# State-by-weight products two quarters at a time beside the scores, and the first batch's first product in plain fp32

## The chip, the cores and the metric

The kernel runs on one core of one Trainium2 chip. The metric is device time in microseconds (us) of one execution; a kernel's time is the median of its runs. Before the change three runs gave 1366.35, 1363.53 and 1366.42 us, a median of 1366.35. The profile shown here is of one more execution, which took 1365.6 us and has a span of 1363.8 us.

## The reference

Two attentions read from each other, and their outputs pass through two gated feed-forward blocks. The weights arrive as 64-bit floats, so the kernel converts them itself.

```python
# x: 8 batches, 8 heads, 512 rows, 64 wide; state: the same with 32 rows
scores = x @ state.T / 8;   a  = softmax(scores);   xread = a @ state
scores2 = state @ x.T / 8;  a2 = softmax(scores2);  sread = a2 @ x
t = concat(xread, sread)                 # per batch 544 rows of 512
h = ((t @ w1) * (t @ w2)) @ w3           # w1, w2: 512 x 1024; w3: 1024 x 1024
y = h @ w_out                            # w_out: 1024 x 512
out = (sigmoid(y @ w_gate) * (y @ w_val)) @ w_out2   # 1536 wide inside
```

## The kernel before

**Split products.** Most products run in the format fp32r, one pass over the moving operand. To keep fp32 accuracy each operand is split into a high part (ACT copies it into an fp32r tile) and a low part (DVE subtracts the high part from the original); `split` (line 65) does both. A product is then three matmuls: high by high, high by low, low by high (`products`, line 114).

**First feed-forward block.** It never forms `xread` for the 512 rows. With `aT` the softmax over the states, transposed, `xread @ w1` is `aT.T` times (state times w1). So for each batch `StateWeights.make(q)` (line 370) multiplies the state by one quarter `q` of w1 and w2: 16 small matmuls of 64 rows by 32 columns that lie side by side in the array (tile `psw`), followed by a split into the tiles `sw`. Two consecutive blocks `j` of `ffn1` (line 444) use one quarter. For each of 8 blocks `j`, `ffn1` forms the two products `pab` (128x512, from `aT` and `sw`), multiplies them (line 470) and splits the result into `u`. Then four products `py` (d = 0 to 3) multiply all `u` by `wp`, which is w3 times w_out, formed once in the first batch (`wp_step`, line 425, tile `pwp`, with transposes of w3 in `pw`).

**The front.** In the first batch everything waits for weights: `convert` (line 332) and `cvt` (line 71) load 64-bit tiles into three buffers `raw`, and ACT and DVE turn each into 32-bit numbers. w1 and w2 take 16 such tiles, w_out 8, w3 16. The converted quarters of w1 and w2 are also written to memory and fetched again for each later batch (`fetch`, tile `wq`, 1 MB each, two buffers).

**What sets the order.** The order on PE is the order in which the program is written (line 160). `ffn1` has slots, 0 to 7 ahead of the blocks `j` and 8 to 11 ahead of `d`, and lines 622 to 673 hang work into them: the next batch's transposes of x (`pxt`), scores (`psc`, `scores`, line 190), softmax (`soft1` to `soft3`, which end in the split of `aT`), the quarters 0 and 1 of the next batch (slots 9 and 10; in the first batch 8 and 11), its quarters 2 and 3 (slots 0 and 3 of the next batch). In the first batch `wp_step(0)` stands in slot 7, ahead of the last block `j`, and the other seven in slot 8. The other engines are ordered by the scheduler. `psw` shares two PSUM tiles (`ps_at`) with the transposes and scores.

**The rest.** After the eighth batch the state rows follow, and then the second feed-forward block, which takes the time from about 585 us to the end.

Of the kernel before, what the change touches and what calls it, by code (L numbers as in the profile page):

```python
# [8 lines left out]
F32 = mybir.dt.float32  # L9
# [12 lines left out]
def tile_state_attention__then__gated_ffns(  # L22
# [137 lines left out]
    with tc.manual_schedule(engines={mybir.EngineType.PE}):  # L160
# [5 lines left out]
        def load_x(b, pool):  # L166
            t = pool.tile([P, G, SC, 2, D], F32, name="xn", bufs=1)
# [6 lines left out]
        def attention(b):  # L174
# [61 lines left out]
            def soft3():  # L236
# [5 lines left out]
                )  # L242
                aT[b] = [at.tile([P, 2, S], F32R, name=f"aT{i}") for i in range(2)]
# [116 lines left out]
        class StateWeights:  # L360
# [9 lines left out]
            def make(self, q):  # L370
                w = self.raw.pop(q)
                b = self.b
                pts = [ps_at.tile([P, 512], F32, tag="at", name="psw") for _ in range(2)]
                for a in range(2):
                    for g in range(G):
                        for k in range(2):
                            nc.tensor.matmul(
                                pts[k][NS * g : NS * g + NS, a * WQ : (a + 1) * WQ],
                                stT[64 * k : 64 * k + 64, g, b * NS : (b + 1) * NS],
                                w[64 * k : 64 * k + 64, a, g],  # L380
                                start=True,
                                stop=True,
                            )
                t = [pb.tile([P, 2, 2, WQ], F32R, name=f"sw{i}", bufs=3) for i in range(2)]
                for k in range(2):
                    split(*[v[:, k].rearrange("p a f -> p (a f)") for v in t], pts[k])
                self.done[q] = t

            def weights(self, j):
                t = self.done[j // 2]  # L390
                f0 = j % 2 * P
                return [[t[i][:, :, a, f0 : f0 + P] for i in range(2)] for a in range(2)]

        order = list(range(B))
        before, after = attention(order[0])
        nxt = StateWeights(order[0])
        stages = [fn for i in sorted(before) for fn in before[i]]
        nxt.raw[0] = convert(0, {1: lambda: load_x(order[0], at)})
# [3 lines left out]
        wo = [pw.tile([P, JF, DM], F32R, name=f"wo{i}", bufs=1) for i in range(2)]  # L402

        def wo_step(k):
            split(wo[0][:, k], wo[1][:, k], cvt(w_out[k * P : (k + 1) * P, :], cv))
# [19 lines left out]
        def wp_step(f):  # L425
# [3 lines left out]
            if f + 1 < JF:  # L429
# [6 lines left out]
                        ([t[:, k % 4] for t in w3t[2 * f + k // 4]], [t[:, k] for t in wo])  # L436
# [7 lines left out]
        def ffn1(c, n, kblocks, weights, xin, slots):  # L444
# [6 lines left out]
            for j in range(JF):  # L451
# [4 lines left out]
                for ab in range(2):  # L456
# [11 lines left out]
                asb = pb.tile([P, 512], F32, name="asb")  # L468
                p2["act"] = copy("act", asb[:, :n], pab[0][:, :n])
                p2["dve"] = nc.vector.tensor_tensor(  # L470
                    out=asb[:, :n], in0=asb[:, :n], in1=pab[1][:, :n], op=ALU.mult
                )
                uj = [pu.tile([P, 512], F32R, name=f"u{i}", bufs=JF) for i in range(2)]
                split(uj[0][:, :n], uj[1][:, :n], asb[:, :n])
                u.append(uj)
# [18 lines left out]
        class DirectWeights:  # L494
# [5 lines left out]
            def prep(self, j):  # L500
# [4 lines left out]
                t = [pb.tile([P, 2, KM, P], F32R, tag=f"sw{i}", name=f"dw{i}", bufs=3) for i in range(2)]  # L505
# [115 lines left out]

        for t, b in enumerate(order):
            cur = nxt
            slots = {i: [] for i in range(JF + KM)}
            if t == 0:
                for q in range(NQ):
                    slots[2 * q].append(lambda q=q, cur=cur: cur.make(q))
# [9 lines left out]
                for f in range(JF):  # L637
                    slots[min(JF, f + WS)].append(lambda f=f: wp_step(f))
# [11 lines left out]
            if t + 1 < B:  # L650
                if t == 0:
                    slots[JF].append(lambda: behind(lambda: load_x(order[1], pu)))
                else:
                    go = lambda t=t: load_x(order[t + 1], at if t % 2 else pu)
                    slots[0].insert(0, (lambda go=go: behind(go)) if t == 1 else go)
                before, after = attention(order[t + 1])
                nxt = StateWeights(order[t + 1])
                for i, fns in before.items():
                    slots[i + 2 if t == 0 else i] += fns
                for q in range(2):  # L660
                    if t == 0:
                        slots[JF].append(lambda q=q, nxt=nxt: behind(lambda: nxt.fetch(q)))
                    else:
                        slots[4].append(lambda q=q, nxt=nxt: nxt.fetch(q))
                    i = (8, 11)[q] if t == 0 else 9 + q
                    slots[i].append(lambda q=q, nxt=nxt: nxt.make(q))
                    slots[i].append(lambda q=q, nxt=nxt: nxt.fetch(q + 2))
# [5 lines left out]
            ffn1(t, S, 2, cur.weights, aT[b], slots)  # L673
# [488 lines left out]
```

## Time and profile before

| | before |
|---|---|
| median of 3 runs | 1366.35 us |
| the profiled execution, its time and its span | 1365.6 us, 1363.8 us |
| PE busy | 1311.1 us (96%) |
| DVE busy, ACT busy | 857.5 us (63%), 681.9 us (50%) |
| end of w3 times w_out, first batch | 143.6 us |
| one later batch (scores to scores) | 54.2 us |

PE is the engine that matters: from about 89 us to the end it hardly ever stands still. Ahead of that it waits for weights. The clock that the throttle granted to PE is 1.00 (the level of 2.4 GHz) in nearly every slice of the span, and lower only between 40 and 100 us.

### The profile page before, as it was taken

To read this page: it belongs to the slowest core of one execution; us is meant where nothing else is said; L and a number is where in the kernel's file an instruction comes from. 1 tells how busy PE (TensorE), PEld (TensorE's weight loads), DVE (VectorE), ACT (ScalarE), POOL (GpSimd) and SP (SyncE) were. 2 spreads that over 40 slices of the span, in tenths; PEclk is the share of its full clock that TensorE was granted. 3 is DMA by queue.
4 is the path that set the end of the run, shared out by engine and by line. 5 is a ranking of instruction groups with operands and counts; after the bars stand their busy time and mean duration, and the time that the engine had idled before them with its cause. 6 is when DMAs were issued, how large, how long until landed. Compare 5 with 4: busy or idle time off the path is not lost. (4 is left out here: it accounts for less than half of the span.)

```text
span 1363.8 us, 20423 instructions
## 1 busy us (share of the span) xinstructions
PE 1311.1 (96%) x7696; PEld 1100.9 (81%) x7696; DVE 857.5 (63%) x1528; ACT 681.9 (50%) x1344; POOL 132.4 (10%) x155
## 2 busy tenths in 40 slices
PE   3769999999999999999999999999999999999997
PEld 1558777777777777988889998888999988889996
DVE  6776354645645558348658776768777756557643
ACT  6775344454544556355646655635545533424431
POOL 0000000010110111002122211121211000000000
PEclk9879999999999999999999999999999999999999
DMA  7847433454464444454244377454465654042222
GB/s 221 296 162 219 138 106 124 125 154 178 143 213 155 155 160 181 182 219 166 101 155 150 133 262 247 184 199 156 164 213 191 237 218 156 28 159 93 82 93 70
DMA packets 125354, 224.68 MB, mean 165 GB/s; under 512 B 44104, under 2 KB 71240, under 8 KB 118600
## 3 DMA queue, kind: packets, MB, share of 16 engines
q1 hardware_dynamic: 90088, 162.95, 35.7%
q10 hardware_dynamic: 33440, 46.80, 10.2%
q0 software_dynamic: 1728, 13.63, 2.5%
q8 instruction: 60, 0.98, 0.3%
q14 instruction: 38, 0.31, 0.1%
HBM read 155.19 MB, written 68.16 MB: 164 GB/s over the span
## 5 line engine op out<-in xcount | busy, mean ns | idle before, releaser
L949 PE MATMUL psA<-y,wt 128*128 128x384 f32 (+1 forms) x1440 | 300.9, 357 | 0.6 <-ACT sg L974 0.5
L1046 PE MATMUL po<-wo,p 128*128 128x512 f32 x1224 | 281.0, 390 | 0.7 <-DVE p L602 0.7
L949 PEld LDWEIGHTS psA<-y,wt 128*128 128x128 f32 x1440 | 259.0, 188 | 24.9 <-DVE sg L985 0.9
L1046 PEld LDWEIGHTS po<-wo,p 128*128 128x128 f32 x1224 | 229.3, 188 | 49.0 <-DVE p L602 1.8
L949 PE MATMUL psB<-y,wt 128*128 128x384 f32 (+1 forms) x720 | 159.6, 356 | 0.0
L123 PE MATMUL pab<-aT,sw 128*128 128x512 f32 x512 | 149.3, 414 | 10.3 <-ACT aT L62 6.6
L62 ACT ACTIVATE u<-psA 128x384 f32<-128x384 f32 (+1 forms) x120 | 63.9, 532 | 156.1 <-PE psA L949 141.5
L949 PEld LDWEIGHTS psB<-y,wt 128*128 128x128 f32 x720 | 130.0, 188 | 11.2
L123 PE MATMUL py<-u,wp 128*128 128x512 f32 (+1 forms) x576 | 133.3, 383 | 1.1 <-DVE u L67 0.6
L123 PEld LDWEIGHTS py<-u,wp 128*128 128x128 f32 x576 | 102.4, 188 | 32.5 <-issue 9.2
L123 PEld LDWEIGHTS pab<-aT,sw 128*128 128x128 f32 x512 | 95.2, 195 | 36.9 <-ACT aT L62 7.5
L62 ACT ACTIVATE p<-sg 128x384 fp32r<-128x384 f32 (+1 forms) x120 | 68.0, 567 | 81.1 <-DVE sg L985 69.8
L67 POOL TENSOR_TENSOR o<-m,o 128x256 fp32r<-128x256 f32 x72 | 60.2, 836 | 435.1 <-ACT o L62 379.8
L470 DVE TENSOR_TENSOR asb<-asb,pab 128x512 f32<-128x512 f32 (+1 forms) x72 | 47.3, 657 | 71.5 <-PE pab L126 61.2
L1061 DVE TENSOR_TENSOR ob<-po,ob 128x512 f32<-128x512 f32 x68 | 46.7, 688 | 63.4 <-PE po L1046 60.2
L976 DVE TENSOR_TENSOR sg<-psB,u 128x384 f32<-128x384 f32 (+1 forms) x60 | 36.4, 607 | 75.1 <-ACT u L62 75.0
L126 PE MATMUL pab<-aT,sw 128*128 128x512 f32 x256 | 81.3, 399 | 0.0
L949 PE MATMUL psC<-y,wt 128*128 128x384 f32 (+1 forms) x360 | 80.2, 357 | 0.0
L67 DVE TENSOR_TENSOR sw<-psw,sw 128x512 fp32r<-128x512 f32 x64 | 41.5, 680 | 56.7 <-ACT sw L62 56.6
L602 DVE TENSOR_TENSOR p<-sg,p 128x384 fp32r<-128x384 f32 (+1 forms) x120 | 73.8, 615 | 3.9 <-ACT p L62 0.8
L602 DVE TENSOR_TENSOR y<-yf,y 128x384 fp32r<-128x384 f32 (+1 forms) x112 | 68.5, 635 | 12.0 <-ACT y L62 10.9
L67 DVE TENSOR_TENSOR u<-asb,u 128x512 fp32r<-128x512 f32 (+1 forms) x72 | 51.8, 719 | 33.5 <-ACT u L62 33.5
(114 smaller groups left out, 1783.2 us busy)
## 6 DMA issues: line engine op xcount, KB each, us to landing
wq<-w12d SPq DMA_DIRECT2D x32, 1024.0 KB, 5.0
wt<-wd SPq DMA_DIRECT2D x12, 1792.0 KB, 9.0
part<-ob SPq DMA_DIRECT2D x68, 256.0 KB, 2.6
ob<-part SPq DMA_DIRECT2D x68, 256.0 KB, 3.8
raw<-in_moe_w SPq DMA_DIRECT2D x32, 512.0 KB, 4.8
wd<-o ACTq DMA_DIRECT2D x56, 256.0 KB, 2.2
yf<-yd SPq DMA_DIRECT2D x27, 384.0 KB, 3.8
yf<-yd SPq DMA_DIRECT2D x19, 512.0 KB, 5.2
```

Of the source, the lines that this page charges most:

```text
L62: return nc.scalar.activation(out=o, in_=i, func=AF.Copy)
L67: (sub or nc.vector).tensor_tensor(out=lo, in0=src, in1=hi.bitcast(F32), op=ALU.subtract)
L123: nc.tensor.matmul(o, w[i], xx[k], start=n == 0 and i + k == 0, stop=False)
L126: nc.tensor.matmul(o, w[1 - late], xx[late], start=False, stop=n == len(pairs) - 1)
L470: p2["dve"] = nc.vector.tensor_tensor(out=asb[:, :n], in0=asb[:, :n], in1=pab[1][:, :n], op=ALU.mult)
L602: nc.vector.tensor_tensor(out=o, in0=x0, in1=x1, op=ALU.subtract)
L949: nc.tensor.matmul(o, w[:, i, kb * P : (kb + 1) * P], xx[kb][h], start=start, stop=i == 1 and kb == 1, skip_group_check=True,)
L976: nc.vector.tensor_tensor(out=t, in0=o, in1=kept[a, what], op=ALU.add)
L1046: nc.tensor.matmul(o, pt[j][i][:, s * P : (s + 1) * P], wot[j][:, h], start=j == js[0] and i + h == 0, stop=j == js[-1] and i == 1,)
L1061: nc.vector.tensor_tensor(out=ob, in0=o, in1=ob, op=ALU.add)
```

## The change

The quarters are made two at a time. In a later batch quarters 0 and 1 follow the scores in slot 8 and quarters 2 and 3 stand in slot 10; all four are ready before the next batch begins. In the first batch quarters 0 and 1 stand in slot 8 behind w3 times w_out, and quarters 2 and 3 in slot 10 behind the scores. Their PSUM tiles come from `ps_main` (four tiles), which `pab` and `pwp` use, and there are four buffers for `sw` rather than three. Fetches go in pairs as well.

For the first batch the state-by-weight tiles and `aT` are left unsplit (`plain`): each `pab` product is two plain fp32 matmuls instead of six fp32r ones, and ACT and DVE copy one `psw` tile each. The product `u` of a block stays whole in `uw`, and its split is put behind all eight `wp_step`, which now stand together in slot 8. x has two buffers in one pool, and the low parts of w_out use the buffers of `sw1`.

```diff
+        if len(groups[0][1][0][0]) == 1:
+            for o, pairs in groups:
+                for n, ((w,), (xx,)) in enumerate(pairs):
+                    nc.tensor.matmul(o, w, xx, start=n == 0, stop=n == len(pairs) - 1)
+            return
...
+                if plain:
+                    aT[b] = [tr]
+                    return
                 aT[b] = [at.tile([P, 2, S], F32R, name=f"aT{i}") for i in range(2)]
                 split(aT[b][0], aT[b][1], tr)
...
-            def make(self, q):
+            def make(self, *qs, plain=False):
...
+                    pool, tag = (ps_y, "y") if plain else (ps_main, "m")
+                    pts = [pool.tile([P, 512], F32, tag=tag, name="psw") for _ in range(2)]
...
+                    if plain:
+                        t = [pb.tile([P, 2, 2, WQ], F32, tag="sw0", name="swp", bufs=4)]
+                        for k, eng in enumerate(("act", "dve")):
+                            copy(eng, t[0][:, k].rearrange("p a f -> p (a f)"), pts[k])
...
+                keep_ = postponed is not None and j < JF - 1
+                whole = (pu.tile([P, 512], F32, tag="u", name="uw", bufs=2 * JF) if keep_ else asb)[:, :n]
...
+                if postponed is not None:
+                    postponed.append(split_u)
+                else:
+                    split_u()
...
                 for f in range(JF):
-                    slots[min(JF, f + WS)].append(lambda f=f: wp_step(f))
+                    slots[JF].append(lambda f=f: wp_step(f))
+                slots[JF].append(lambda: [fn() for fn in postponed])
...
-            if t:
-                slots[0].append(lambda cur=cur: cur.make(2))
-                slots[3].append(lambda cur=cur: cur.make(3))
...
+                    slots[JF].append(lambda nxt=nxt: nxt.make(0, 1))
+                    slots[JF].append(lambda get=get: get(2, 3))
+                    for i, fns in before.items():
+                        slots[i + 2] += fns
+                    slots[JF + 2].insert(1, lambda nxt=nxt: nxt.make(2, 3))
+                else:
+                    slots[0].append(lambda get=get: get(0, 1))
...
+                    slots[JF].insert(1, lambda nxt=nxt: nxt.make(0, 1))
+                    slots[JF].append(lambda get=get: get(2, 3))
+                    slots[JF + 2].append(lambda nxt=nxt: nxt.make(2, 3))
```

PE in the first batch, around the last block `j` (its weights are `sw_597` before, `swp` now; `pw` is a transpose of w3, `pwp` w3 times w_out). Before:

```order
L260 MATMUL psr<-xn,a2tr 32x64 x32
...
L126 MATMUL pab<-aT_223,sw_598 128x512 x2
L310 MATMUL pt<-ident,z 128x128 x4
L421 MATMUL pw_748<-ident,m 128x128 x4
L421 MATMUL pw_766<-ident,m 128x128 x4
L421 MATMUL pw_784<-ident,m 128x128 x4
...
L126 MATMUL pwp<-wo_227,w3t_772 128x512 x4
L123 MATMUL pab<-aT_223,sw_597 128x512
...
L421 MATMUL pw_850<-ident,m 128x128 x4
```

After the change (two matmuls for each `pab`):

```order
L268 MATMUL psr<-xn,a2tr 32x64 x32
L122 MATMUL pab<-a2tr,swp 128x512 x4
L318 MATMUL pt<-ident,z 128x128 x4
L438 MATMUL pw_667<-ident,m 128x128 x4
L438 MATMUL pw_685<-ident,m 128x128 x4
L438 MATMUL pw_703<-ident,m 128x128 x4
L128 MATMUL pwp<-wo_223,w3t_672 128x512
...
L131 MATMUL pwp<-wo_223,w3t_691 128x512 x4
L438 MATMUL pw_748<-ident,m 128x128 x4
```

The last block's products moved ahead of the first transposes of w3, and no `pab` stands between the sets of `pwp` any more.

PE in a later batch, from the scores on (`psc`; `py` is a product with `wp`). Before, one set of `psw` stands alone at each place:

```order
L126 MATMUL pab<-aT_1439,sw_1624 128x512 x2
L199 MATMUL psc<-xT,stT 32x512 x8
L123 MATMUL py<-u_1547,wp_82 128x512
...
L126 MATMUL py<-u_1798,wp_83 128x512
L377 MATMUL psw<-wq,stT 32x256 x16
```

After:

```order
L131 MATMUL pab<-aT_1443,sw_1398 128x512 x2
L204 MATMUL psc<-xT,stT 32x512 x8
L387 MATMUL psw<-wq,stT 32x256 x32
L128 MATMUL py<-u_1505,wp_82 128x512
...
L131 MATMUL py<-u_1728,wp_83 128x512
```

Two sets of 16 follow the scores without another product in between; the two others stand together in front of d = 2.

DVE in the first batch, from the scores of the second on (`st` and `m` belong to the softmax, `aT` ends it, `sw` is the low part of a quarter). Before:

```order
L223 TENSOR_REDUCE m_1399<-st 128x32
...
L224 TENSOR_TENSOR st<-st,m_1399 128x1024
...
L231 TENSOR_REDUCE s_1432<-st 128x32
...
L234 TENSOR_TENSOR st<-st,m_1431 128x1024
L67 TENSOR_TENSOR sw_1462<-psw,sw_1461 128x512
L240 STREAM_TRANSPOSE a2tr<-st 128x1024
...
L67 TENSOR_TENSOR aT_1440<-a2tr,aT_1439 128x1024
```

After:

```order
L67 TENSOR_TENSOR sw_1374<-psw,sw_1373 128x512
...
L228 TENSOR_REDUCE m_1403<-st 128x32
...
L67 TENSOR_TENSOR sw_1398<-psw,sw_1397 128x512 x2
L229 TENSOR_TENSOR st<-st,m_1403 128x1024
L236 TENSOR_REDUCE s_1436<-st 128x32
...
L239 TENSOR_TENSOR st<-st,m_1435 128x1024
L245 STREAM_TRANSPOSE a2tr<-st 128x1024
L67 TENSOR_TENSOR aT_1444<-a2tr,aT_1443 128x1024
```

Four subtractions of `sw` now stand ahead of the softmax's own subtraction (`st<-st,m`), where before two stood behind it.

## Rows read from the trace of the kernel before

**Rows 1.** The page, part 1: busy time of each engine, its share, instructions.
```profile
PE 1311.1 (96%) x7696; PEld 1100.9 (81%) x7696; DVE 857.5 (63%) x1528; ACT 681.9 (50%) x1344; POOL 132.4 (10%) x155
```

**Rows 2.** Busy time by stretch (count), then PE's granted clock, DMA share, GB/s.
```profile
33.00:89.00 56.00, 36.28 (x266) 26.70 (x267) 45.82 (x92) 41.20 (x73) 1.82 (x3) 0.83 0.73 249
89.00:97.00 8.00, 8.00 (x29) 6.47 (x28) 5.73 (x12) 5.57 (x9) 0.00 (x0) 0.71 0.64 221
97.00:144.00 47.00, 47.00 (x237) 39.40 (x236) 26.88 (x51) 23.48 (x41) 0.00 (x0) 1.00 0.69 203
```

**Rows 3.** Waits up to 145 us: PE's line, who ended it; total, times, longest.
```profile
PE pw L421 <- DVE m L112: 7.9, 3, 6.0
PE psr L260 <- DVE sw L67: 4.1, 1, 4.1
```

**Rows 4.** PE in order of time, second batch: start, length, instruction (merged).
```profile
205.29 1.98 PE L126 MATMUL py<-u,wp 128*128 128x512 f32 x8
207.19 1.21 PE L377 MATMUL psw<-wq,stT 64*32 64x256 f32 x32
208.33 3.96 PE L123 MATMUL py<-u,wp 128*128 128x512 f32 x16
212.13 1.97 PE L126 MATMUL py<-u,wp 128*128 128x512 f32 x8
...
220.77 3.79 PE L123 MATMUL py<-u,wp 128*128 128x512 f32 x16
224.40 1.98 PE L126 MATMUL py<-u,wp 128*128 128x512 f32 x8
226.31 1.09 PE L377 MATMUL psw<-wq,stT 64*32 64x256 f32 x32
227.33 1.20 PE L123 MATMUL pab<-aT,sw 128*128 128x512 f32 x4
228.36 0.62 PE L126 MATMUL pab<-aT,sw 128*128 128x512 f32 x2
```

**Rows 5.** The tile wq: us from issue to landing of its transfers.
```profile
DMA to landing us min/median/max: 4.6/5.1/7.8
```

**Rows 6.** Groups of instructions by form: busy us, mean ns; idle time before them.
```profile
L67 DVE TENSOR_TENSOR u<-asb,u 128x512 fp32r<-128x512 f32 x64 | 48.4, 756 | 32.1 <-ACT u L62 32.0
L67 DVE TENSOR_TENSOR sw<-psw,sw 128x512 fp32r<-128x512 f32 x64 | 41.5, 680 | 56.7 <-ACT sw L62 56.6
L63 DVE COPY ob<-po 128x512 f32<-128x512 f32 x17 | 11.7, 688 | 11.7 <-PE po L1046 11.6
L199 PE MATMUL psc<-xT,stT 64*32 64x512 f32 x128 | 10.3, 658 | 0.0
L67 DVE TENSOR_TENSOR aT<-a2tr,aT 128x1024 fp32r<-128x1024 f32 x8 | 9.8, 1224 | 3.8 <-ACT aT L62 3.8
```

**Rows 7.** PE in order of time, first batch.
```profile
73.45 2.08 PE L123 MATMUL pab<-aT,sw 128*128 128x512 f32 x4
...
84.42 1.12 PE L421 MATMUL pw<-ident,m 128*128 128x128 f32 x4 [6.04 <-DVE m L112]
...
89.29 5.97 PE L123 MATMUL pwp<-wo,w3t 128*128 128x512 f32 x16
...
96.91 1.07 PE L123 MATMUL pab<-aT,sw 128*128 128x512 f32 x4
```

**Rows 8.** Waits of all engines up to 100 us.
```profile
DVE r L101 <- DMA raw<-in_moe_w: 13.0, 7, 6.0
```

**Rows 9.** All engines in order of time, end of the first batch.
```profile
158.68 1.09 PE L199 MATMUL psc<-xT,stT 64*32 64x512 f32 x16
...
170.68 0.65 DVE L67 TENSOR_TENSOR sw<-psw,sw 128x512 fp32r<-128x512 f32 x1
...
171.87 1.23 DVE L67 TENSOR_TENSOR aT<-a2tr,aT 128x1024 fp32r<-128x1024 f32 x1 [0.55 <-ACT aT L62]
...
173.09 1.20 PE L123 MATMUL pab<-aT,sw 128*128 128x512 f32 x4
```

More of the change, by code (lines that the diff above doesn't have):

```diff
@@ L172, in load_x, with attention @@
             xn[b] = t
-        def attention(b):
+        def attention(b, plain=False):
             t = {}
@@ L391, in weights @@
                 f0 = j % 2 * P
-                return [[t[i][:, :, a, f0 : f0 + P] for i in range(2)] for a in range(2)]
+                return [[v[:, :, a, f0 : f0 + P] for v in t] for a in range(2)]
         order = list(range(B))
-        before, after = attention(order[0])
+        before, after = attention(order[0], True)
         nxt = StateWeights(order[0])
         stages = [fn for i in sorted(before) for fn in before[i]]
-        nxt.raw[0] = convert(0, {1: lambda: load_x(order[0], at)})
+        nxt.raw[0] = convert(0, {1: lambda: load_x(order[0])})
         state_turn(0)
@@ L401, in tile_state_attention__then__gated_ffns @@
             fn()
-        wo = [pw.tile([P, JF, DM], F32R, name=f"wo{i}", bufs=1) for i in range(2)]
+        wo = pw.tile([P, JF, DM], F32R, name="wo0", bufs=1)
+        wol = [pb.tile([P, 2, DM], F32R, tag="sw1", name="wol", bufs=4) for _ in range(JF // 2)]
+        wo = [(wo[:, k], wol[k // 2][:, k % 2]) for k in range(JF)]
         def wo_step(k):
-            split(wo[0][:, k], wo[1][:, k], cvt(w_out[k * P : (k + 1) * P, :], cv))
+            split(*wo[k], cvt(w_out[k * P : (k + 1) * P, :], cv))
         w3f = ahead(
@@ L435, in wp_step @@
                     [
-                        ([t[:, k % 4] for t in w3t[2 * f + k // 4]], [t[:, k] for t in wo])
+                        ([t[:, k % 4] for t in w3t[2 * f + k // 4]], wo[k])
                         for k in range(JF)
@@ L441, in wp_step, with ffn1 @@
             split(wp[0][:, f], wp[1][:, f], po)
-        def ffn1(c, n, kblocks, weights, xin, slots):
+        def ffn1(c, n, kblocks, weights, xin, slots, postponed=None):
             u = []
@@ L504, in prep @@
                 f = self.raw[q][:, :, :, jj * P : (jj + 1) * P]
-                t = [pb.tile([P, 2, KM, P], F32R, tag=f"sw{i}", name=f"dw{i}", bufs=3) for i in range(2)]
+                t = [pb.tile([P, 2, KM, P], F32R, tag=f"sw{i}", name=f"dw{i}", bufs=4) for i in range(2)]
                 for a in range(2):
@@ L620, in first_y @@
                     ys[0][o][kb] = t
+        postponed = []
         for t, b in enumerate(order):
@@ L626, in tile_state_attention__then__gated_ffns @@
                 for q in range(NQ):
[L627 removed]
+                    slots[2 * q].append(lambda q=q, cur=cur: cur.make(q, plain=True))
                     if q + 1 < NQ:
@@ L650, in tile_state_attention__then__gated_ffns, with get @@
             if t + 1 < B:
[L651 to L655, printed above, removed]
+                go = lambda t=t: load_x(order[t + 1])
+                slots[JF if t == 0 else 0].append((lambda go=go: behind(go)) if t < 2 else go)
                 before, after = attention(order[t + 1])
                 nxt = StateWeights(order[t + 1])
[L658 to L667, printed above, removed]
+                def get(*qs, nxt=nxt):
+                    for q in qs:
+                        nxt.fetch(q)
+                if t == 0:
+                    slots[JF].append(lambda get=get: behind(lambda: get(0, 1)))
+                    slots[JF].append(lambda nxt=nxt: nxt.make(0, 1))
[3 more added lines that the diff above has]
+                    slots[JF + 2].insert(1, lambda nxt=nxt: nxt.make(2, 3))
+                else:
+                    slots[0].append(lambda get=get: get(0, 1))
+                    for i, fns in before.items():
+                        slots[i] += fns
+                    slots[JF].insert(1, lambda nxt=nxt: nxt.make(0, 1))
+                    slots[JF].append(lambda get=get: get(2, 3))
+                    slots[JF + 2].append(lambda nxt=nxt: nxt.make(2, 3))
             else:
@@ L672, in tile_state_attention__then__gated_ffns @@
                 slots[JF].append(open_c1)
-            ffn1(t, S, 2, cur.weights, aT[b], slots)
+            ffn1(t, S, 2, cur.weights, aT[b], slots, postponed if t == 0 else None)
         xs = [p2["pool"].tile([P, KM, NSR], F32R, name=f"xs{i}", bufs=1) for i in range(2)]
```

43 lines of the change are left out of this document (22 added, 21 removed).

## The prediction

> **What bounds the kernel now.** I read the page first, then a table of stretches, PE's waits, and PE's instructions in order of time at the two places that the change touches. PE is busy 96% of the span [rows 1]. It stands still almost only ahead of 89 us: between 33 and 89 us it is busy 36.28 of 56 us, so 19.7 us are idle; from 97 to 144 us, while w3 times w_out is formed, it is busy throughout [rows 2]. So there are two kinds of place. In the front, PE waits for ACT and DVE, which convert weights: the longest wait there, 6.0 us, is for the first transposes of w3 [rows 3]. From then on time is saved only by giving PE less to do, and lost only by making it wait.
>
> **Sets of state-by-weight products side by side.** An undisturbed run of 16 full products takes 3.63 us (220.77 to 224.40), 0.227 us each [rows 4]. The set of `psw` at 207.19 costs more than itself. The 8 products ahead of it end at 205.29 + 8 x 0.227 = 207.11; the set lasts to 208.33; and the next 16 products take 3.80 us instead of 3.63. That is 0.08 + 1.14 + 0.17 = 1.39 us. The set ahead of `pab` at 226.31 costs 0.09 + 1.02 + 0.12 = 1.23 us, the last term because 4 products take 1.03 us (227.33 to 228.36) instead of 0.91 [rows 4]. A batch has two of each kind and one set of scores, which reads like the cheaper kind: 2 x 1.39 + 3 x 1.23 = 6.47 us. After the change there are two blocks: scores and two sets, 3 x 1.02 + 0.23 = 3.29 us, and two sets within `py`, 2 x 1.02 + 0.37 = 2.41 us, together 5.70 us. The difference is 0.77 us a batch, and there are seven batches whose quarters are made so: 5.4 us. Bounds: nothing, if a set behind another of its kind pays its edges all the same; and 7.8 us, if a set that follows another takes 0.91 us, the time of four products of full width [rows 4], so that three times 0.11 us more go in each batch.
>
> The Trainium skill ("TensorEngine Tiling (Array Packing)", Key Properties) says that changing the tiling mode drains the engine, and "TensorE: Matmul & The Clock Gate" (Single matmul latency) puts a drain near 175 ns. By that six changes of mode fewer would be 1.05 us a batch, an estimate, and 7.4 us in all; the edges above, 0.21 to 0.25 us for two changes, say less.
>
> **What these sets now wait for.** Quarters 2 and 3 are fetched when the first two have been multiplied, and are wanted two `py` later, 2 x 24 x 0.227 = 10.9 us. A transfer of `wq` landed 4.6 to 7.8 us after its issue [rows 5]. On SP nothing else of that batch stands behind them that is wanted sooner. I take nothing. Four PSUM tiles of `ps_main` are needed at once; the last one comes free when DVE has multiplied the last `pab`, 0.7 us after it ended, and the scores and one set (2.0 us) run meanwhile: nothing again.
>
> **The front.** Removed from DVE ahead of w3 are the split of `aT` (1.22 us), four of eight operations on the first batch's quarters (8 subtractions of 0.68 us become 4 copies, which I price like the copy from PSUM, 0.69 us), and seven splits of `u` (0.76 us each): 1.22 + 2.7 + 5.3 = 9.2 us [rows 6]. ACT loses about as many operations. Added on PE: 32 plain products instead of 96 fp32r ones. The trace has no plain product of full size. Its scores are plain: 16 records for 8 matmuls, so two per matmul, of 658 ns each [rows 6], eight side by side in a set of 1.02 us. So a plain 128x512 product costs between two full passes, 0.455 us, and 1.02 us; I take 0.95, near the upper one because the set's time holds its start. Then PE has 32 x 0.95 - 96 x 0.227 = 8.6 us more (bounds -7.2 and +10.8), 6.4 of it ahead of block 6, where it fits into the 19.7 us of idle time.
>
> When does w3 times w_out start? PE's first transposes of w3 stood at 84.42 and the first product at 89.29 [rows 7]. They may not come before block 7 now: block 6 began at 73.45 and blocks 6 and 7 take 8 x 0.95 = 7.6 us, so PE itself is ready at about 81.5, 2.9 us earlier than 84.42. The conversions may allow up to 9.2 us, or nothing if the transfers set the pace (DVE waited 13.0 us for tiles of w1, w2 and w3 to land [rows 8]). I take 3.0 us earlier, what PE allows.
>
> From there to the end of w3 times w_out, before: a first set of 7.6 us (89.29 to 96.91) at a granted clock of 0.71, block 7 with 12 x 0.227 = 2.7 us, and seven further sets [rows 2, 7]. Block 7 leaves this stretch: -2.7 us. A set of 24 at full clock is 5.45 us, so up to 2.2 us of slow clock can go; block 7 now runs shortly ahead, but 3 us of waiting stay in between, and I take 0.5. The 16 postponed splits of `u` lie beside the sets: DVE is busy 26.88 of 47 us there and gets 6.1 more [rows 2, 6]. Three stand behind each other in one set at places, so I take 0.5 us of waiting (bounds 0 and 2). The front: -3.0 - 2.7 - 0.5 + 0.5 = -5.7 us.
>
> The Trainium skill ("FP8 and Floating Point Precision", TensorE Precision Notes) says that true fp32 takes four passes. That speaks against the change, which pays four for three; four times 0.227 would be 0.91 us a product, an estimate, and blocks 6 and 7 would end 0.3 us sooner than I reckon.
>
> **A new wait, once.** In the first batch the scores stand two `py` ahead of the second batch's `pab`, as before. Then the softmax ended at 171.87 + 1.23 = 173.10 and the first `pab` stood at 173.09 [rows 9]: no slack. The distance on PE stays: three sets and 10.9 us are 14.3, where 14.41 were. But DVE now runs four subtractions of `sw` ahead of the softmax's own, where two stood behind, one of them in a gap (170.68, while ACT copied `aT`) [rows 9]. That is 4 x 0.68 - 0.68 = 2.0 us more in the chain [rows 6], and some 0.6 us because ACT must first copy the high parts between its exponentials. PE waits 2.6 us, once (bounds 0 and 4). In later batches 22 us lie between and nothing waits.
>
> **Sum.** -5.4 - 5.7 + 2.6 = -8.5 us, against the profiled execution's 1365.6: 1357.1. The median of the runs is 0.75 us above that execution, so I forecast 1357.9 us.
>
> **Rivals.**
> - *Transfers pace the front.* The first set of w3 times w_out starts no earlier and stays slow, and only block 7's move remains: -2.7 + 0.5 in the front, 1366.35 - 2.2 + 2.6 - 5.4 = 1361.4. For it: DVE's waits for landings. Against: they are shorter than the relief, and an earlier release of a buffer lets the next load go earlier.
> - *Sets pay their edges all the same.* 1366.35 - 5.7 + 2.6 = 1363.3. For it: nothing in the trace shows two sets in a row. Against: between them no instruction of another form stands.
> - *More goes than I take.* All upper bounds (-9.2 - 2.7 - 2.2 - 7.8, no new wait) would be 1344; half way, 1351.
> - *Slower: the plain products run at the slow clock.* The granted clock was 0.83 between 33 and 89 us [rows 2]. At 1.2 GHz all along a plain product costs 1.9 us; 32 are 39 us more than 21.8, and 19.7 us of idle time cannot hide it: the front ends about 19 us later. 1366.35 + 19 - 2.7 - 5.4 + 2.6 = 1380. It decides from 0.68 + 19.7 / 32 = 1.3 us a product on. For it: PE still stops and starts there. Against: it stops less, since each pair of blocks keeps it busy for 7.6 us on end.
>
> **How the numbers follow.** Forecast 0.60 (its own range 1354 to 1361.3); transfers 0.16; more 0.12; edges 0.07; slow clock 0.05. Leaving out the slow clock and the lower half of the case with more, the range is 1350.5 to 1363. A change of 0.2%, 2.7 us, is what a measurement of this kernel can tell, so faster means under 1363.6: the forecast, transfers, more, and a half of edges, 0.60 + 0.16 + 0.12 + 0.03, of which I take 0.04 off for what I have not thought of: 0.87. Same: 0.07. Slower: 0.06.
>
> **What would show it.** Right: `psw` sets in pairs with about 1.02 us each and one edge; records of plain `pab` products near 0.47 us; the end of w3 times w_out near 138 us instead of 143.6; one wait of PE for `aT` of 2 to 3 us ahead of the second batch; a batch of 53.4 us instead of 54.2. Wrong: PE waiting for `wq` or `psw` in the middle of a batch, or w3 times w_out ending after 143 us.

## The result and the profile after

The changed kernel takes 1351.07 us (median of 4 runs, 1350.89 to 1353.18), beside 1365.91 us before (4 runs): a ratio of 0.9898, 95% interval 0.9881 to 0.9915. It is faster, by 14.8 us, where 8.5 us were forecast. The time lies inside the stated range of 1350.5 to 1363, near its lower end and below the 1354 to 1361.3 that the forecast had as its own; the direction and the places were right, and the size of the sets' term was not.

The page, part 1, of the kernel after (engine, busy us, share, instructions). PE has 9.3 us less to do than in [rows 1], although 32 plain products cost more than the 96 that they replace; the rest of the 14.7 us of span is waiting that went.

```profile
PE 1301.8 (96%) x7664; PEld 1092.5 (81%) x7664; DVE 854.3 (63%) x1523; ACT 677.2 (50%) x1339; POOL 132.6 (10%) x155
```

The kernel after in the stretches of [rows 2]: between 33 and 89 us PE is busy 44.54 us instead of 36.28, and from 89 to 144 us its granted clock is full.

```profile
33.00:89.00 56.00, 44.54 (x269) 22.06 (x268) 44.35 (x89) 41.53 (x72) 1.60 (x3) 0.90 0.77 261
89.00:97.00 8.00, 8.00 (x45) 6.67 (x44) 7.33 (x15) 6.34 (x12) 0.00 (x0) 1.00 0.61 185
97.00:144.00 47.00, 46.86 (x284) 37.55 (x283) 27.20 (x50) 24.08 (x44) 0.00 (x0) 1.00 0.74 228
```

PE of the kernel after in order of time, the front (start, length, instruction, and the idle time before it with its releaser). The transposes of w3 (`pw`) stand at 79.43 instead of 84.42 and the first product `pwp` at 84.01 instead of 89.29 [rows 7], 5.3 us earlier. The first set of w3 times w_out lasts 5.57 us, to 89.58, where it took 7.6.

```profile
31.48 10.10 PE L122 MATMUL pab<-a2tr,swp 128*128 128x512 f32 x16 [10.98 <-DVE a2tr L245]
...
49.72 3.60 PE L122 MATMUL pab<-a2tr,swp 128*128 128x512 f32 x8
53.24 1.09 PE L387 MATMUL psw<-wq,stT 64*32 64x256 f32 x32
...
59.68 9.67 PE L122 MATMUL pab<-a2tr,swp 128*128 128x512 f32 x16 [4.76 <-ACT swp L62]
69.28 1.09 PE L387 MATMUL psw<-wq,stT 64*32 64x256 f32 x32
...
79.43 0.60 PE L438 MATMUL pw<-ident,m 128*128 128x128 f32 x4
80.57 0.63 PE L438 MATMUL pw<-ident,m 128*128 128x128 f32 x4 [0.54 <-DVE m L112]
83.60 0.66 PE L438 MATMUL pw<-ident,m 128*128 128x128 f32 x4 [2.40 <-DVE w3t L67]
84.01 0.47 PE L128 MATMUL pwp<-wo,w3t 128*128 128x512 f32 x1
...
89.58 1.03 PE L438 MATMUL pw<-ident,m 128*128 128x128 f32 x8
```

A plain product, two records, costs (53.24 - 49.72) / 4 = 0.88 us at full clock. At that price 16 records are 7.04 us; those from 31.48 on took 10.03 us and those from 59.68 on 9.6. Ahead of both PE had just stood still, and the granted clock was down: 0.70 from 31 to 42 us, 0.76 from 60 to 70 us.

The end of the first batch, same kernel, same view. PE waits for `aT`, 1.26 and 0.76 us, and then its products are slow: four take 1.71 us (167.77 to 169.48) instead of 0.91. Without either, `pa` would stand 8 + 12 products of 0.227 us behind 161.77, at 166.31; it stands at 170.33, 4.0 us later.

```profile
149.81 1.09 PE L204 MATMUL psc<-xT,stT 64*32 64x512 f32 x16
150.69 1.93 PE L387 MATMUL psw<-wq,stT 64*32 64x256 f32 x64
...
161.77 1.98 PE L131 MATMUL py<-u,wp 128*128 128x512 f32 x8
165.01 0.50 PE L128 MATMUL pab<-aT,sw 128*128 128x512 f32 x1 [1.26 <-ACT aT L62]
166.26 0.96 PE L128 MATMUL pab<-aT,sw 128*128 128x512 f32 x3 [0.76 <-DVE aT L67]
...
167.77 1.91 PE L128 MATMUL pab<-aT,sw 128*128 128x512 f32 x4
169.48 1.05 PE L131 MATMUL pab<-aT,sw 128*128 128x512 f32 x2
170.33 0.75 PE L258 MATMUL pa<-ident,e 128*128 128x128 f32 x4
```

Where the slow products run, the table of stretches (length, busy PE, PEld, DVE, ACT, POOL, then the granted clock) has a granted clock of 0.50, the lower of the two levels (1.2 GHz). Two other executions of this kernel, further below, have the same wait without it.

```profile
168.00:170.30 2.30, 2.30 (x6) 1.64 (x6) 0.00 (x0) 0.60 (x1) 0.00 (x0) 0.50 0.03 7
```

A later batch of the kernel after, where [rows 4] showed lone sets. Two sets (`psw` x64) follow the scores, two stand between two `py`. From one batch's scores to the next are 246.62 - 193.78 = 52.84 us, where it was 54.22.

```profile
193.78 1.09 PE L204 MATMUL psc<-xT,stT 64*32 64x512 f32 x16
194.67 1.93 PE L387 MATMUL psw<-wq,stT 64*32 64x256 f32 x64
196.53 3.94 PE L128 MATMUL py<-u,wp 128*128 128x512 f32 x16
200.31 1.98 PE L131 MATMUL py<-u,wp 128*128 128x512 f32 x8
...
205.75 1.97 PE L131 MATMUL py<-u,wp 128*128 128x512 f32 x8
207.65 1.96 PE L387 MATMUL psw<-wq,stT 64*32 64x256 f32 x64
209.54 3.96 PE L128 MATMUL py<-u,wp 128*128 128x512 f32 x16
213.34 1.98 PE L131 MATMUL py<-u,wp 128*128 128x512 f32 x8
...
246.62 1.09 PE L204 MATMUL psc<-xT,stT 64*32 64x512 f32 x16
```

The path of PE in milestones (us of these two profiled executions; in other executions of the changed kernel, further below, the second batch's scores come up to 4.2 us later):

| start of | before | after | difference | gained in the stretch |
|---|---|---|---|---|
| first product of w3 times w_out | 89.29 | 84.01 | -5.3 | -5.3 |
| scores for the second batch | 158.68 | 149.81 | -8.9 | -3.6 |
| scores for the third batch | 200.49 | 193.78 | -6.7 | +2.2 |
| second FFN | 582.3 | 566.9 | -15.4 | -8.7 |
| (span) | 1363.8 | 1349.1 | -14.7 | +0.7 |

### The profile page after: what moved, and what is told of

The parts are those of the page before. It is cut to its first block, busy times and chain, and to the rows that moved or that the text cites. A ratio compares the mean times of both kernels' runs of the same rounds, so it can differ in the third digit from the quotient of the medians.

```text
span 1349.1 us, 20318 instructions
## 1 busy us (share of the span) xinstructions
PE 1301.8 (96%) x7664; PEld 1092.5 (81%) x7664; DVE 854.3 (63%) x1523; ACT 677.2 (50%) x1339; POOL 132.6 (10%) x155
## 5 line engine op out<-in xcount | busy, mean ns | idle before, releaser
L128 PE MATMUL pab<-aT,sw 128*128 128x512 f32 x448 | 125.5, 402 | 2.0 <-ACT aT L62 1.3
L489 DVE TENSOR_TENSOR asb<-asb,pab 128x512 f32<-128x512 f32 (+1 forms) x65 | 42.5, 655 | 108.7 <-PE pab L131 99.5
L128 PEld LDWEIGHTS pab<-aT,sw 128*128 128x128 f32 x448 | 81.6, 189 | 19.1 <-ACT aT L62 1.7
L94 ACT ACTIVATE r<-raw 128x512 uint16<-128x512 uint32 (+1 forms) x100 | 64.0, 641 | 12.4 <-DMA raw<-in_moe_w 4.1
L980 PEld LDWEIGHTS psC<-y,wt 128*128 128x128 f32 x360 | 64.8, 188 | 6.4 <-DVE s L1013 0.8
L131 PE MATMUL pab<-aT,sw 128*128 128x512 f32 x224 | 70.0, 394 | 0.0
```

What stands on the lines that cost most here:

```text
L94: nc.scalar.activation(out=r.bitcast(U16).rearrange("p (f t) -> p f t", t=2)[:, :, 0], in_=lo, func=AF.Copy, scale=2.0**-29,)
L489: p2["dve"] = nc.vector.tensor_tensor(out=whole, in0=asb[:, :n], in1=pab[1][:, :n], op=ALU.mult)
L980: nc.tensor.matmul(o, w[:, i, kb * P : (kb + 1) * P], xx[kb][h], start=start, stop=i == 1 and kb == 1, skip_group_check=True,)
```

## Experiments

Every time stands beside the kernel before on the same chip, which took 1367.45 to 1367.87 us there; ratios are to it, with 95% intervals. Three groups: the sets, the front, the wait.

**The front alone, sets as before.** From the second batch on, quarters are made one by one again, in the old pool and at the old places.

```diff
-    pool, tag = (ps_y, "y") if plain else (ps_main, "m")
+    pool, tag = (ps_y, "y") if plain else (ps_at, "at")
...
-    slots[JF].insert(1, lambda nxt=nxt: nxt.make(0, 1))
...
-    slots[JF + 2].append(lambda nxt=nxt: nxt.make(2, 3))
...
+    slots[i].append(lambda q=q, nxt=nxt: nxt.make(q))
```

> The changed kernel with only its front (plain first batch, u split later, w3 times w_out behind block 7); from the second batch on the four quarters are made one by one, in the pool and at the places of the kernel before. My theory: the two parts of the change add up. The changed trace has the start of the second batch's scores 6.7 us earlier than before, and each later batch 1.39 us shorter. Then this kernel has batches of 54.2 us again, the end of w3 times w_out near 134.4 us as in the changed kernel, and a time near 1351.1 + 6 x 1.4 = 1359.5 us; 1358 if the wait for aT before the second batch becomes shorter, since fewer subtractions of sw stand ahead of the softmax on DVE. Rival, the front does it all and the batches became shorter because DVE or ACT have less pressure or buffers differ (four of each sw, x in another pool): batches stay at 52.8 to 53.3 us and the time at 1351 to 1354.

Measured: 1361.26 us, ratio 0.9954 (0.994 to 0.9969), 6.4 us faster than before; batches of 54.24 us: without the joined sets a batch is as long as before, and the rival falls. The wait for `aT` is gone too, as one of the cases had it: from the scores to the first `pa` of the second batch are 17.27 us, where the changed kernel has 20.52. But that case had 1358 us, and the ratio alone would give 1359.6. Summed up, 6.4 for the front and 10.5 for the sets (from the milestones), less 2.6 to 4.0 for the wait, are 12.9 to 14.3 us, where the whole change brings 14.8; the gap is inside the interval of this run, about 2 us on each side. This kernel's lone set between two `py`: 1.14 us to the next product, as in [rows 4].

```profile
198.64 1.21 PE L387 MATMUL psw<-wq,stT 64*32 64x256 f32 x32
199.78 3.96 PE L128 MATMUL py<-u,wp 128*128 128x512 f32 x16
```

**The changed kernel, its sets apart.** Four blocks a batch instead of two, all from `ps_main`.

```diff
-    slots[JF].insert(1, lambda nxt=nxt: nxt.make(0, 1))
-    slots[JF].append(lambda get=get: get(2, 3))
-    slots[JF + 2].append(lambda nxt=nxt: nxt.make(2, 3))
+    for q in range(4):
+        slots[JF + q].insert(1 if q == 0 else 0, lambda q=q, nxt=nxt: nxt.make(q))
+        if q < 2:
+            slots[JF + q].append(lambda q=q, get=get: get(q + 2))
```

> The changed kernel; from the second batch on the four quarters for the next batch are made one at a time, each in its own place between products (the first still beside the scores), from the same PSUM pool: four blocks of such products in a batch instead of two. My theory, the edges of a block: the three blocks that went between before and after took 6.47 - 5.12 = 1.35 us, 0.45 each, so two more blocks cost 0.9 us a batch, batches of 53.7 us, and 6 x 0.9 = 5.4 us in all: 1356.5. Each lone set again takes 1.02 us from the first of its records to the next product. Rival, the other PSUM pool (ps_main instead of ps_at) or the place is what made the batches shorter: batches stay at 52.8 us, the time at 1351 (within 1 us). By the term as forecast, 0.23 us per pair of edges, 2 x 0.23 x 6 = 2.8 us: 1353.9.

Measured: 1356.07 us, ratio 0.9922 (0.9907 to 0.9936); the changed kernel's is 0.989. Batches of 53.55 us: two more blocks cost 0.72 us, 0.36 each, between the 0.45 of my theory and the 0.23 of the forecast's term. The rival (nothing but pool and place) falls. But the lone set between two `py` was cheaper here than in the kernel before: 1.02 us, and the next 16 products 3.76, so 0.08 + 1.02 + 0.13 = 1.23 us instead of 1.39.

```profile
201.89 1.09 PE L387 MATMUL psw<-wq,stT 64*32 64x256 f32 x32
202.91 3.92 PE L128 MATMUL py<-u,wp 128*128 128x512 f32 x16
206.67 1.98 PE L131 MATMUL py<-u,wp 128*128 128x512 f32 x8
```

**The kernel before, its later sets from the other PSUM pool.** This asks where the 0.16 us between 1.39 and 1.23 come from.

```diff
-    pts = [ps_at.tile([P, 512], F32, tag="at", name="psw") for _ in range(2)]
+    pool, tag = (ps_at, "at") if b == order[0] else (ps_main, "m")
+    pts = [pool.tile([P, 512], F32, tag=tag, name="psw") for _ in range(2)]
```

> The kernel before, in which from the second batch on the sets of state-by-weight products take their PSUM tiles from ps_main instead of ps_at; each set stays alone at its old place. In the variant with four sets apart, from ps_main, a lone set among py cost 1.23 us, where before it cost 1.39; that is 0.32 us of a batch which joining does not explain. Theory pool: the two sets among py cost 1.23 us here too, batches 53.9 us instead of 54.22, the time 2 us less (ratio 0.9985). Rival, the pool does nothing and the difference lies in what stands around the set (the work of DVE and ACT beside it): batches stay 54.22 us and the time within 1 us. The theory that the pool made the whole gain of a batch, 52.9 us, would need 1.3 us here.

Measured: 1364.8 us, ratio 0.9975 (0.9965 to 0.9984), 3.1 us faster; batches of 53.94 us, 0.28 less, as the theory of the pool had it. Seven batches of that are 2.0 us. One batch of the kernel before is 54.68 us long instead of 54.22, which no batch is here; where the rest of the 3.1 comes from is open. The set shrinks from 1.21 to 1.09 us at its old place:

```profile
206.89 1.09 PE L378 MATMUL psw<-wq,stT 64*32 64x256 f32 x32
207.91 3.92 PE L123 MATMUL py<-u,wp 128*128 128x512 f32 x16
```

So of a batch's 1.39 us the pool gives 0.28, and joining 1.11. The trace shows why: it is a wait for a tile, inside the set. A set writes two PSUM tiles in turn, and `ps_at` has only two, which the scores use as well. In the kernel before, the set at 207.19 begins in a tile that is free; the other one is still read by the softmax of the scores, until 207.07 + 0.19 = 207.26. Up to 207.30 only one record of the set has begun. At the set from 214.04 on it is DVE's subtraction on the quarter made just before, which ends at 213.47 + 0.65 = 214.12; up to 214.17 one record has begun:

```profile
207.07 0.19 ACT L213 ACTIVATION_READ_ACCUMULATOR e<-psc,m 128x1 f32 x1
207.19 0.40 PE L377 MATMUL psw<-wq,stT 64*32 64x256 f32 x1
213.47 0.65 DVE L67 TENSOR_TENSOR sw<-psw,sw 128x512 fp32r<-128x512 f32 x1
214.04 0.40 PE L377 MATMUL psw<-wq,stT 64*32 64x256 f32 x1
```

From `ps_main`, eight have begun within 0.08 us (up to 206.97):

```profile
206.89 0.45 PE L378 MATMUL psw<-wq,stT 64*32 64x256 f32 x8
```

That is the 0.12 us between 1.14 and 1.02, and somewhat more in the second set (1.16). No table of waits has it, because PE counts as busy once the first record runs. Ahead of `pab` no record of the set waits, and there a set from `ps_at` takes 1.02 us too [rows 4].

**The plain products alone.** The front alone, but u split at once and the first set of w3 times w_out ahead of block 7. The change's other buffers (x, the low parts of w_out, four for `sw`) stay.

```diff
-    slots[JF].append(lambda f=f: wp_step(f))
+    slots[min(JF, f + WS)].append(lambda f=f: wp_step(f))
...
-    ffn1(t, S, 2, cur.weights, aT[b], slots, postponed if t == 0 else None)
+    ffn1(t, S, 2, cur.weights, aT[b], slots, None)
```

> Of the change the plain products of the first batch alone: u is split at once, the first set of w3 times w_out stands ahead of block 7, and later batches make their quarters one by one as before. My theory: plain products take PE 6.6 us more (32 x 0.887 instead of 96 x 0.227), and DVE and ACT have four splits and that of aT less to do; in the front the one about pays for the other, with part of the plain products at the lower granted clock (16 records in 10 us instead of 7). The other two edits of the front then bring most of it: splitting u later some 3 us, block 7 ahead some 3.5. I expect 1 to 3 us less than before, ratio 0.998 to 0.9995. Rival: the plain products bring the whole gain of the front (8 us less than before in the variant with the front alone): ratio 0.994 to 0.9955. Rival, slower: the plain products at the lower clock delay the front, ratio over 1.002.

Measured: 1368.66 us, ratio 1.0006 (0.9997 to 1.0016). No gain at all, where 1 to 3 us less were expected: plain products by themselves turn PE's idle time into work and no more. PE waits for w3 as it did, and the first set starts at 90.18 (89.29 before):

```profile
75.74 5.40 PE L122 MATMUL pab<-a2tr,swp 128*128 128x512 f32 x8 [2.96 <-ACT swp L62]
...
86.03 0.63 PE L438 MATMUL pw<-ident,m 128*128 128x128 f32 x4 [4.46 <-DVE m L112]
...
90.18 0.78 PE L128 MATMUL pwp<-wo,w3t 128*128 128x512 f32 x1
```

**The other two edits without the plain products.** The kernel before, u split later and the first set of w3 times w_out behind block 7.

```diff
-    slots[min(JF, f + WS)].append(lambda f=f: wp_step(f))
+    slots[JF].append(lambda f=f: wp_step(f))
+    slots[JF].append(lambda: [fn() for fn in postponed])
...
+    if postponed is not None:
+        postponed.append(split_u)
```

> The kernel before (first batch in three products of high and low parts, as there), with two edits of the front alone: u split behind w3 times w_out, and the first set of w3 times w_out behind block 7. Of the change it has neither the plain products nor the sets side by side. The plain products alone gave nothing (ratio 1.0006), and the variant with the whole front 0.9954; this one tells whether the two edits need the plain products. My theory: DVE and ACT bound the front, and PE's 6.6 us more of plain products lie in its idle time; what the plain products take off DVE ahead of w3 (the split of aT and four subtractions on quarters, 3.9 us) comes back only where block 7 no longer stands behind w3. So without them the front gains 2 to 4.5 us instead of 6.3, ratio 0.9967 to 0.9985. Rival: the plain products give nothing here either, the two edits give it all, ratio 0.9954 or less. Rival: without the plain products the edits give nothing, ratio 0.9995 or more.

Measured: 1363.46 us, ratio 0.9966 (0.9953 to 0.9978), 4.0 us faster. As expected, between the rivals, and by a small margin: its interval just includes the rival's 0.9954. In its trace the first set starts at 89.61 and runs slow (5.79 us for 16 products), as before; only block 7's 2.7 us have moved into PE's wait. So in these runs the plain products, worth nothing alone, add some 2 us to the other two edits; since the intervals of this variant and of the whole front meet, that size is not settled. (By the two profiles w3 times w_out ends at 141.26 us here and at 135.09 with the whole front, but this execution was the slowest of its variant and that one the fastest.)

**Block 7 behind the first set again.** The changed kernel with the first change of the variant of the plain products alone (`slots[min(JF, f + WS)]`).

> The changed kernel, with the first set of w3 times w_out again ahead of block 7 of the first batch's first product, as before. My theory: conversions on DVE and ACT, not PE, set when that set can start (84.0 us in the changed kernel, after waits of 0.5 and 2.4 us for w3), so it starts no earlier here, PE stands still for the 3.5 us of block 7's plain products longer ahead of it, and block 7 comes behind: 3 to 4.5 us more (the granted clock falls again in the first set), ratio 0.992 to 0.993. Rival, PE sets the start, as the prediction reckoned: the first set starts 3.5 us earlier, and the time stays within 1 us of the changed kernel's.

Measured: 1355.99 us, ratio 0.9915 (0.99 to 0.993), 3.2 us more than the changed kernel's 1352.79 beside it. PE has no block 7 to do ahead of the first product, which comes at 84.77 (84.01 and 86.69 in the changed kernel's first two profiles) after 2.02, 0.98 and 1.03 us of waiting for DVE: conversions set the start, not PE. The first set then takes 8.0 us, to 92.79, and block 7 stands behind:

```profile
80.77 0.63 PE L438 MATMUL pw<-ident,m 128*128 128x128 f32 x4 [2.02 <-DVE m L112]
82.38 0.63 PE L438 MATMUL pw<-ident,m 128*128 128x128 f32 x4 [0.98 <-DVE m L112]
84.03 1.09 PE L438 MATMUL pw<-ident,m 128*128 128x128 f32 x4 [1.03 <-DVE m L112]
84.77 0.78 PE L128 MATMUL pwp<-wo,w3t 128*128 128x512 f32 x1
...
92.79 3.59 PE L122 MATMUL pab<-a2tr,swp 128*128 128x512 f32 x8
```

**u split at once.** The changed kernel with only the last change of that same variant (`ffn1(..., None)`).

> The changed kernel, but in the first batch u is split into its two parts right after each block, as before, instead of after w3 times w_out. My theory: the conversions on DVE set when the first set of w3 times w_out can start, so seven splits of 0.76 us more ahead of it, partly beside DVE's waits for transfers, start it 2.5 to 5.3 us later, and the time is 1353.5 to 1356.5; the granted clock of the first set falls again. Some 0.5 to 0.8 us come back because the splits no longer stand beside the sets of w3 times w_out. Rival, PE's own plain products (8 x 0.9 us for blocks 6 and 7) set it, as the prediction reckoned: the start stays within 1 us and the time within 1 us of 1351.

Measured: 1356.37 us, ratio 0.9918 (0.9906 to 0.9931), 3 to 4 us more than the changed kernel by its ratios of 0.989 to 0.9898. PE waits three times for w3 again, all for DVE (1.03, 1.25, 1.51 us), and the first product comes at 92.35. Against 84.01 that is later than the theory's 2.5 to 5.3 us, but against the 86.69 and 87.09 of the kernel's other profiles it is not by much, and in this execution block 6 was late as well (77.36, beside 72.02 in the first profile of the changed kernel and 73.83 in the last), which it may owe to the splits or to the execution. The time is the better measure, and it is inside what was expected. The wait for `aT` is here too (1.26 and 0.76 us), at a granted clock of 1.00 behind it.

**The second batch's attention one product earlier.** In the first batch alone; quarters 2 and 3 then stand behind the softmax.

```diff
+                    slots[JF] += before[6]
...
-                    for i, fns in before.items():
-                        slots[i + 2] += fns
-                    slots[JF + 2].insert(1, lambda nxt=nxt: nxt.make(2, 3))
+                    slots[JF] += before[7]
+                    slots[JF + 1] += before[8]
+                    slots[JF + 2].append(lambda nxt=nxt: nxt.make(2, 3))
+                    slots[JF + 2] += before[9]
```

> The changed kernel; in the first batch alone the steps of the second batch's attention stand one product earlier on PE (its scores behind the first py instead of beside the second), and quarters 2 and 3 are made behind the softmax instead of ahead of it. Nothing else moves. My theory: the wait for aT ahead of the second batch's first pab (1.26 + 0.76 us of waiting) and the 1.7 us by which the products after it run slower go together, because the lower granted clock follows the stop: 3.7 us less, 1347.4 us; second batch's products at 0.227 us from the first on. Rival A, the lower clock there has another cause: only the 2.0 us of waiting go, 1349.1, and the first products of the second batch take 1.9 us for 4 as before. Rival B, something else comes late instead (quarters 2 and 3, now behind the softmax on DVE, or the transposes of the second batch's x): 1351, with a wait for sw or x in place of that for aT.

Measured: 1350.23 us, ratio 0.987 (0.9854 to 0.9886). The second batch's products run at full speed from the first on, no wait for `aT` and no slow clock:

```profile
167.07 1.07 PE L128 MATMUL pab<-aT,sw 128*128 128x512 f32 x4
167.97 0.62 PE L131 MATMUL pab<-aT,sw 128*128 128x512 f32 x2
```

The interval meets that of the changed kernel, so both ran again on one chip.

> The changed kernel with the second batch's attention one product earlier in the first batch, once more, beside the changed kernel on one chip. If the wait for aT with the slow products behind it costs 3.6 us of PE's path (20.52 us from the scores to the fifth product of the second batch, against 16.92 with one more py between), this is 2.5 to 3.6 us faster than the changed kernel, ratio 0.9870 to 0.9875. Rival: the front's other variations eat it, within 1 us of the changed kernel.

> The changed kernel itself, beside the variant with earlier scores: ratio 0.989 to 0.990, with the wait for aT.

Measured: 1349.77 us (1349.0 to 1350.58), ratio 0.9867 (0.9853 to 0.988), and 1353.48 us (1352.07 to 1353.96), ratio 0.9891 (0.9876 to 0.9906). The runs do not overlap: 3.7 us by the medians. Neither profile of this version has the wait or a slow clock behind it, so rivals A and B fall. What part of the gain is the clock's is not shown: the changed kernel's profile beside it has the wait (1.26 and 0.76 us) and a granted clock of 1.00 behind it. By these two profiles 2.5 us go between the end of w3 times w_out and the third batch's scores (57.82 and 55.30 us). This version is faster than both kernels.

**The changed kernel again**, beside the variants of the pool and of block 7.

> The changed kernel itself once more, so that the variants stand beside it on one chip. If nothing but the chip differs, its ratio to before is again 0.990, within 0.988 to 0.992, batches of 52.83 us and a wait for aT of 2.0 us ahead of the second batch.

Measured: 1352.79 us, ratio 0.989 (0.9873 to 0.9907), batches of 52.83 us, as expected. Two things differ from the first profile. The front was slower: the first product of w3 times w_out stands at 86.69 instead of 84.01, and at 87.09 in the execution of the pair above. In all seven profiles with this front it lies between 83.91 and 87.09, and in the two with the front before at 89.29 and 89.96; so it comes 2.2 to 6.0 us earlier, and the table above shows a good execution.

And the same wait for `aT` was not followed by a slow clock. The products behind it take 0.92 us for four, and `pa` stands at 171.96, 2.6 us behind what 20 products from 164.80 on would give, where the first profile had 4.0:

```profile
164.80 1.98 PE L131 MATMUL py<-u,wp 128*128 128x512 f32 x8
168.03 0.49 PE L128 MATMUL pab<-aT,sw 128*128 128x512 f32 x1 [1.25 <-ACT aT L62]
...
170.57 1.08 PE L128 MATMUL pab<-aT,sw 128*128 128x512 f32 x4
171.49 0.63 PE L131 MATMUL pab<-aT,sw 128*128 128x512 f32 x2
171.96 0.60 PE L258 MATMUL pa<-ident,e 128*128 128x128 f32 x4
```

Six profiles have this wait, with the same two pieces. In three of them a stretch at a granted clock of 0.50 follows, and from the scores to `pa` are 20.5 to 20.7 us (the first profile, block 7 behind the first set, sets apart); in three the clock stays at 1.00, and there are 19.1 us (this one, that of the pair, u split at once). What decides between them no run here shows.

## Why the prediction was right, and where its sizes failed

*Sets side by side: forecast -5.4 us (0 to -7.8), measured -10.5.* By the milestones: -8.7 us from the third batch's scores to the second FFN, and -1.8 before it, which is the +2.2 of that stretch less the 4.0 of the wait. What a batch's sets cost before was read rightly, 6.47 us. After, the two blocks cost (0.09 + 0.89 + 1.86 + 0.15) + (0.08 + 1.89 + 0.17) = 5.13 us, not 5.70.

The term that was mis-sized: "scores and two sets, 3 x 1.02", and "two sets within `py`, 2 x 1.02 + 0.37". The 1.02 us of a lone set hold part of its edges; inside a block a set takes 0.89 to 0.95, which makes 0.46 of the 0.57 us. The forecast had this as its upper bound (0.91 for a set that follows another). The other 0.11 are in the 0.37, the edges taken over from a lone set between two `py`: 0.12 of them were no edge but the wait for a tile of `ps_at`, which is gone with `ps_main`. The forecast asked whether `ps_main` would have a free tile, not whether `ps_at` had had one; row against row (1.21 and 1.09 us, [rows 4]) the difference stood there, put down to the neighbours. By the runs a batch's 1.39 us are 1.11 from joining and 0.28 from the pool, and seven batches 9.7 of the 10.5 us; the rest is open.

The estimate from the Trainium skill ("TensorEngine Tiling (Array Packing)", Key Properties, with the drain of "TensorE: Matmul & The Clock Gate", Single matmul latency) was 1.05 us a batch for six changes of mode; the 1.11 us measured for joining agree with it, better than the reading of the lone edges did.

*The front: forecast -5.7 us, measured -8.9 in the profiled execution, -5.8 and -4.7 in the other two profiles of the same kernel (scores for the second batch at 152.84 and 154.02), each against the one profile before.* So the forecast's sum lies among the executions. Start of w3 times w_out: -5.3, -2.6 and -2.2, where -3.0 was taken. The reason given was wrong all the same: "I take 3.0 us earlier, what PE allows." In the first profile PE was there at 79.43 instead of the reckoned 81.5, and still waited 2.9 us for DVE's w3; in the other two it waited 3.0 and 1.4 us. What sets the start is the conversions, as block 7's variant and that of u show, each some 3 us slower; that 3.0 came near is luck. The bound of 9.2 us had the right mechanism; why only 2 to 5 of it came was not tried.

What follows is the first profile's sum. Block 7 no longer stands in the stretch: -2.7, as reckoned. Slow clock of the first set: 7.6 became 5.57 us, -2.0 instead of -0.5 (6.7 and 5.6 us in the other two profiles, 8.0 with block 7 behind it). These three are 10.0 us and 8.9 came out. The seven further sets took 6.40 us each (89.58 to 134.38) instead of 6.29, 0.8 in all, where 0.5 was taken for the postponed splits; yet PE is busy 46.86 of 47 us there, so that it is they is not shown. (The forecast's "16 postponed splits" are 16 operations, eight splits; its 6.1 us of DVE are reckoned for eight.) The last 0.4 us or so are a second set of state-by-weight products that now stands ahead of the scores.

*The plain products: forecast 0.95 us, measured 0.88.* The estimate from the Trainium skill's four passes ("FP8 and Floating Point Precision", TensorE Precision Notes), 0.91, was nearer. The slower rival did happen in part: two runs of 16 records took some 3 and 2.6 us more, at granted clocks of 0.70 and 0.76 around them. It decided nothing: the plain products alone, with such stretches too, came out at 1.0006.

*The new wait: forecast +2.6 us, measured +4.0 in the first profile and +2.6 in the other two.* The place and the mechanism were right. From the scores to the end of `aT` are 16.40 us (149.81 to 166.21), where 14.42 were, 2.0 more, as four subtractions ahead of the softmax's own make it; in the front alone they are 14.43 again.

```profile
164.99 1.22 DVE L67 TENSOR_TENSOR aT<-a2tr,aT 128x1024 fp32r<-128x1024 f32 x1 [1.12 <-ACT aT L62]
```

The 0.6 us that the forecast added for ACT's order did not come. But PE's own way got as much shorter by the joined sets, 13.8 us (149.81 to 163.59) instead of the 14.3 reckoned, so the 2.6 came out by luck. What it did not price is what can follow a wait: in the first profile PE then ran 2.3 us at a granted clock of 0.50, and `pa` came 1.4 us later than in the other two. So it was, by about as much, in three of the six profiles with this wait.

*Rivals.* That transfers pace the front falls with the start that came 2.2 to 5.3 us earlier and with the variant of u, whose splits on ACT and DVE alone delay it; that sets pay their edges all the same falls with 52.83 us a batch. The result is that of "more goes than I take", 1351, but not by its reason (no new wait): the wait came, and joining and pool paid for it.

Priced at nothing and rightly so: `wq` landed 4.7 to 9.5 us after its issue, and PE never waited for it in a later batch.

## What to carry to other kernels

Small-tile products cost less in one block than alone, and the duration of a lone set, from its first record to the next product, already holds part of what a neighbour would save; take it as an upper bound of a joined one. When two rows of the same work differ by a tenth of a microsecond, look at the single records: here it was a wait for a PSUM tile inside a block, which no table of waits shows. When pricing a wait, count how much earlier the waiting engine itself arrives (0.6 us here), and add, as a case of its own, a stretch at the lower clock behind it (1.4 us more here, in half of the profiles). Read a term from more than one execution before explaining it: the front's differed by 4 us. Work taken off busy converters and given to an idle TensorE was worth nothing by itself (1.0006), while 4.0 us came from moving what else stood in the converters' and TensorE's way: first ask which wait ends last.

## What was not expected of the hardware

A stop of PE in two pieces, 1.26 and 0.76 us, was followed by 2.3 us at a granted clock of 0.50, though the clock had been at 1.00 from 89 us to the stop. In three of six profiles with this same stop the clock stayed at 1.00. In the seven profiles without such a stop it stays at 1.00 from 98 to 1340 us.
